# RWKV-7 recurrence and a gelu MLP on one core: a new order for tasks 157 to 655 of a hand-written list

## The chip, the cores and the metric

The kernel runs on one core of a Trainium2 chip, in float32. The metric is device time in microseconds; before and after are compared by the median of their runs. The engines are TensorE (PE, with its weight loads as PEld), VectorE (DVE), ScalarE (ACT), GpSimd (POOL) and SyncE (SP), which issues nearly all transfers.

## The reference

For 4 batches and 8 heads, a 40 x 40 state is carried through 768 steps; the outputs of all heads, brought to 3072 tokens of 320 channels, pass through an MLP of width 2048 with the quick gelu.

```python
for t in range(S):
    y[:, :, t] = np.einsum('bhd,bhde->bhe', rt, state)
    Sa = np.einsum('bhde,bhe->bhd', state, at)
    state_decay = state * wt[:, :, None, :] - np.einsum('bhd,bhe->bhde', Sa, bt)
    state = state_decay + np.einsum('bhd,bhe->bhde', vt, kt)
...
h = x @ w_in
g = h * (1.0 / (1.0 + np.exp(-1.702 * h)))
return (g @ w_out)
```

## The kernel before

**Units and chunks.** Time is cut into 12 chunks of 64 steps. A unit is one chunk for two of the four batches, so there are 24 units; unit i is chunk i // 2. For each unit, `decay` (L548) makes running products of w by logarithm, sum and exponential, `prep` (L623) scales k, a, b and makes the score matrices A (L640) and RV (L652), `inverse` (L672) inverts a triangular system in five levels (`level`, L746, and for the first four units `plain_level`, L768), and `solve` (L846) takes the state in from two units before, solves (`solved`, L909), reads out y (`read`, L923) and makes the new state (`updated`, L940) and the unit's x (`decayed`, L956). x goes to DRAM (`part_with`, L971) and comes back transposed by its layout (`get_back`, L977). There is one buffer for x on its way out (L282), so a unit's x cannot be written before that of the unit before has landed in DRAM.

**The MLP.** Once both units of a chunk have come back, `mlp` (L987) multiplies by w_in (`up`, L990, ten tasks for each of four pairs q), applies gelu on ACT (`gelu`, L999), and multiplies by w_out (`down`, L1004, eight tasks for each of two halves). The MLP's matmuls are most of PE's work, and they serve as filler between the steps of the recurrence, which depend on one another. But the MLP of chunk 0 cannot begin before units 0 and 1 are done.

**The weights.** w_in and w_out arrive as 64-bit words in eight slices (L441), four transfers each. Each slice is put together by one pass on ACT (`rebased`, L455), three on DVE (`bounded`, `shifted`, `rounded`, L459 to L467) and one on POOL (`joined`, L471), through a few staging places that are used again. Slices 0 to 3 serve `up` of q 0 to 3, slices 4 to 7 serve `down`.

**The order.** Every step is a task; the program numbers them as it makes them (L65). In which order they are emitted, and so the order of each engine's own queue, is a list written out in `ORDER` (L109 to L246). A token is the task's number, the letter of its engine (p PE, a ACT, d DVE, g POOL, s SP) and a digit: for tasks that use PSUM, which of the four pairs of banks they use (L295), for transfers, how many may be under way (the window, L332; 0 for any number). `listed` (L89) reads the list and marks where ACT must load another activation table (L102). An engine works its queue in order and waits where an input, a buffer or a PSUM pair is not ready. Two engines that read one PSUM tile do so one after the other. All matmuls carry line L301, all transfers on SP line L331, whichever task they belong to.

The tasks that the prediction speaks of, by number:

| task | what it is |
|---|---|
| 139, 140 | x of unit 0 to DRAM, and back |
| 189, 190, 191, 193 | unit 1: X (`solved`), its mask to M, y (`read`), x (`decayed`) |
| 194, 195 | x of unit 1 to DRAM, and back |
| 344 | RV's load for unit 3, window 2 |
| 53, 60 | pieces of w_out |
| 319, 351, 353, 360, 363, 302 | B0 of unit 2, A3 and RV3 (scores of unit 3), L11 and L13 (levels 0 and 1 of unit 3), L18 (last level of unit 2) |
| 196 to 205, 207 to 216 | `up` of chunk 0, q 0 and q 1 |
| 330, 331 and 400, 401 | x of units 2 and 3 to DRAM, and back |
| 552 | wc's load for unit 8, into the buffer that unit 5's exponentials read |
| 82, 549 | `rebased` of the last slice; exponentials of unit 5 |
| 570, 571, 537 | preset of PT for unit 5; N5 (its scores); B1 of unit 4 |
| 498, 578, 503 | L20, L21, L22: levels 0 of units 4 and 5 and level 1 of unit 4 |
| 610, 566, 694 | zT of unit 5; A5; sums over time of unit 6 |
| 402 to 411 | `up` of chunk 1, q 0, the first that need x of unit 3 |

Of the kernel before, what the change touches and what calls it, by code (L numbers as in the profile page):

```python
# [109 lines left out]
0s 8s 1s4 5s 102a 7s 6s 3a 9s 157a 87p0 88p1 10s 89a1 100p2 90a0 95d 13s4 4a 11s 93d 12s 101d2 98p3 2s 94d 97d 17s 103p1 16s 96d  # L110
142p0 15s 104a1 105d1 141p2 143a0 106d 99d3 107p1 144a2 18s4 148g 132p3 108a1 109d1 155p0 45s4 149d 27s 150g 156d0 158p2 14s4
110p1 159a2 160d2 91s4 130p0 161d 19a 24s4 112d1 162p2 111a1 22d 26s4 25s 163a2 113p1 20d 131a0 152g 164d2 34s4 92a 272s 21d
165p0 114a1 151g 271s 147a 153p2 115d1 273s 166a0 167d0 116p1 23g 28a 154d2 262p0 343s 117d1 263p2 133a3 342s 264a2 118d1 168p3
36s 31d 33s 119p1 276g 169a3 170d3 35s 120d1 42s 122a1 171p2 277d 278g 121a 43s 124d1 123a1 126p3 173d2 125a1 127d3 285a 29d
128p1 172a2 44s4 286p3 30d 54s4 37a 174p2 129d1 32g 51s4 288d3 134p1 178a2 146s4 175d2 145s 265a0 135d1 176a 187p0 289d 136p1
275s4 179a2 266g 61s 38d 138d1 188a0 341s 139s 287a3 181p0 39d 185p3 40d 137a1 177a2 290p1 313d 180a2 182a0 53s4 280g 279g 274s
186a3 183p2 292d1 281p0 291a1 333p3 41g 184d2 332p1 282d0 189p2 334a3 60s4 345s 314p0 190d2 316a0 346d 355a 191p3 347d 315d0
193d3 356p2 344s2 62s 140s 194s 195s4 192d3 293p0 335a1 358d2 46a 283p3 359d 317p1 294a0 295d0 349g 318a1 284d3 360p0 269a 348d
350g 296p1 336d 361a0 362d0 319p3 383d 357a2 297a1 298d1 384p0 321p2 49d 320a3 299p1 385a0 47d 322a2 63s4 363p3 300a1 301d1
323d2 386a0 302p1 364a3 365d3 353p0 351p2 306a1 48d 267s3 207p3 52s3 307a1 305d1 208p3 50g 268s3 64a 303d1 209p3 352d2 210p3  # L120
211p3 354d0 308a1 196p2 304a 212p3 65d 197p2 213p3 72s3 214p3 70s3 270d 55a 309p1 337s3 198p2 69s4 366p0 310a1 66d 199p2 367a0
# [120 lines left out]
2677p0 2653a3 2654p2 2655p2 2656p2 2657p2 2658p2 2659p2 2660p2 2661p2 2662p2 2663p2 2678p0 2664a2 2665p1 2666p1 2667p1 2668p1  # L242
2669p1 2670p1 2671p1 2672p1 2673p1 2674p1 2679p0 2675a1 2680p0 2681p0 2682p0 2683p0 2687p3 2684d0 2685d0 2688p3 2686s 2689p3
2690p3 2691p3 2692p3 2693p3 2694p3 2698p1 2695a3 2699p1 2696d3 2700p1 2697s 2701p1 2702p1 2703p1 2704p1 2705p1 2706d1 2707d1
2708s
# [904 lines left out]
```

## Time and profile before

| | us |
|---|---|
| median of three runs (lowest to highest) | 680.3 (678.17 to 682.07) |
| span of the profiled execution | 677.7 |
| PE busy | 649.6 |
| DVE busy | 449.7 |
| ACT busy | 329.1 |
| POOL busy | 175.7 |

The profile is of one execution. The page gives its span, from the first to the last instruction, and no separate time for what lies around it. An engine's busy time is the time in which at least one of its instructions ran. The groups "idle before, releaser" tell how long an engine had been idle and what ended that. In a row of the timeline stand the start, the time until the last of the merged instructions ended, engine, line, operation, tiles, shape, count, and in brackets the idle time before it. In a row of the waits stand who waited, for whom, the sum in us, how often, and the longest. In the view by stretches a row holds the stretch, its length, and each engine's busy time, then the granted TensorE clock, the DMA engines' busy share and GB/s.

### The profile page before, as it was taken

What the parts mean: (1) busy time and instruction counts of PE and PEld (TensorE: products, weight loads), DVE (VectorE), ACT (ScalarE), POOL (GpSimd) and SP (SyncE); (2) the same over time, 40 slices, a digit from 0 to 9 for tenths busy, and PEclk for the clock granted to TensorE, in tenths of its full rate; (3) what the DMA queues carried; (4) which work ended last, traced back from release to release, by engine and by line L of the source; (5) the groups of instructions that cost most, each with busy time, mean ns of one, the idle gap of its engine ahead of it and who ended that gap; (6) DMA issues with size and microseconds to landing.
All of it is one profiled execution on the core that took longest, in us unless ns stands there. A gap on an engine that the chain in (4) does not pass through costs nothing.

```text
span 677.7 us, 42447 instructions
## 1 busy us (share of the span) xinstructions
PE 649.6 (96%) x19616; PEld 568.7 (84%) x19616; DVE 449.7 (66%) x916; ACT 329.1 (49%) x681; POOL 175.7 (26%) x201
## 2 busy tenths in 40 slices
PE   5777999999999999999999999999999999999997
PEld 4667787787999997888888899999889798799896
DVE  5777779777867668757776687868656766675001
ACT  3676745634564655654545445455344454263010
POOL 6541443324123123123113211322411421300000
PEclk9979999999999999999999999999999999999999
DMA  6875753415324314432404513513412411200200
GB/s 208 295 255 160 226 172 97 129 42 152 107 64 131 94 58 124 114 107 65 124 14 131 149 35 108 155 33 107 140 38 62 130 53 45 69 15 14 60 13 21
DMA packets 35473, 69.74 MB, mean 103 GB/s; under 512 B 5472, under 2 KB 14816, under 8 KB 35296
## 3 DMA queue, kind: packets, MB, share of 16 engines
q1 hardware_dynamic: 35216, 66.99, 32.9%
q8 instruction: 154, 2.52, 1.6%
q14 instruction: 23, 0.19, 0.1%
q10 hardware_dynamic: 80, 0.04, 0.0%
HBM read 59.15 MB, written 7.86 MB: 99 GB/s over the span
## 4 chain that ended last, share of the span: by engine, by line
PE 88%; DMA 6%; DVE 2%; issue 1%; SPq 1%; ACT 1%; DVEq 0%; ACTq 0%
PE ps_up L301 31%; PE ps_down L301 29%; PE ps_level L301 8%; PE ps_y L301 5%; PE ps_B L301 4%; PE ps_X L301 2%; PE ps_N L301 2%; PE ps_rz L301 1%; PE ps_RV L301 1%; PE ps_A L301 1%; PE ps_zT L301 1%; SPq L331 1%; DMA w_sb<-in_w_in 1%; PE ps_cum L301 1%; PE ps_T L301 1%
## 5 line engine op out<-in xcount | busy, mean ns | idle before, releaser
L301 PE MATMUL ps_up<-xT_all,w_sb 64*64 64x256 f32 x3840 | 253.3, 377 | 2.1 <-issue 1.3
L301 PE MATMUL ps_down<-w_sb,g 64*64 64x320 f32 (+1 forms) x3200 | 241.5, 419 | 0.2 <-ACT zr L879 0.2
L301 PEld LDWEIGHTS ps_up<-xT_all,w_sb 64*64 64x64 f32 x3840 | 170.8, 133 | 18.8 <-issue 2.1
L301 PEld LDWEIGHTS ps_down<-w_sb,g 64*64 64x64 f32 x3200 | 142.5, 133 | 31.6 <-issue 0.4
L1000 ACT ACTIVATE g<-ps_up 128x1024 f32<-128x1024 f32 x48 | 49.2, 1025 | 46.3 <-PE ps_up L301 45.8
L719 POOL TENSOR_TENSOR EX<-ES,quads 128x512 f32<-128x512 f32 x30 | 39.7, 1324 | 116.4 <-DVE ES L712 77.7
L761 ACT COPY W<-ps_level 128x512 f32<-128x512 f32 x56 | 32.8, 585 | 67.7 <-PE ps_level L301 66.0
L301 PEld LDWEIGHTS ps_level<-W,EX 64*64 64x64 f32 x2560 | 60.0, 134 | 5.4 <-DVE T L840 0.2
L763 DVE TENSOR_TENSOR E<-two,ps_level 128x256 f32<-128x256 f32 x80 | 33.1, 415 | 36.5 <-ACT W L761 32.3
L301 PE MATMUL ps_level<-W,EX 64*64 64x64 f32 (+1 forms) x2560 | 56.8, 217 | 0.0
L717 ACT ACTIVATE EX<-ES,quads 128x256 f32<-128x256 f32 x82 | 37.2, 501 | 31.9 <-DVE ES L712 31.3
L629 POOL TENSOR_TENSOR ak<-ak,FT 128x512 f32<-128x512 f32 x17 | 23.0, 1353 | 77.2 <-DMA ak<-in_ak 54.4
L301 PEld LDWEIGHTS ps_level<-PT,EX 64*64 64x64 f32 x1280 | 30.7, 138 | 11.5 <-DVE EX L733 3.3
L301 PE MATMUL ps_level<-PT,EX 64*64 64x64 f32 (+2 forms) x1280 | 32.5, 234 | 6.9 <-DVE EX L733 5.0
L712 DVE STREAM_TRANSPOSE ES<-E 128x256 f32<-128x256 f32 x80 | 35.3, 443 | 4.4
L301 PE MATMUL ps_y<-RV,kh 64*64 64x104 f32 (+1 forms) x768 | 35.4, 247 | 0.9 <-DVE M L917 0.9
L301 PE MATMUL ps_y<-M,bh 64*64 64x104 f32 (+1 forms) x768 | 35.5, 247 | 0.7 <-DVE M L917 0.5
L901 ACT COPY B<-ps_B 128x416 f32<-128x416 f32 (+1 forms) x35 | 17.2, 493 | 34.4 <-PE ps_B L301 34.2
L301 PEld LDWEIGHTS ps_y<-RV,kh 64*64 64x64 f32 x768 | 29.6, 133 | 3.2 <-DVE M L917 1.5
L917 DVE TENSOR_TENSOR M<-ps_X,later 128x832 f32<-128x832 f32 (+1 forms) x24 | 23.9, 995 | 10.2 <-PE ps_X L301 10.0
L301 PE MATMUL ps_B<-RV,A 64*64 64x104 f32 (+1 forms) x768 | 29.2, 252 | 0.8 <-issue 0.8
L637 POOL TENSOR_TENSOR kh<-time,G 128x320 f32<-128x320 f32 x18 | 16.2, 901 | 51.2 <-PE ps_y L301 34.6
(133 smaller groups left out, 1099.0 us busy)
## 6 DMA issues: line engine op xcount, KB each, us to landing
ak<-in_ak SPq DMA_DIRECT2D x48, 160.0 KB
rv<-in_rv SPq DMA_DIRECT2D x48, 160.0 KB
time<-in_time SPq DMA_DIRECT2D x24, 320.0 KB
xT_all<-x_dram SPq DMA_DIRECT2D x48, 160.0 KB
wc<-in_wc SPq DMA_DIRECT2D x20, 264.0 KB
logw<-in_w SPq DMA_DIRECT2D x24, 160.0 KB
RV<-in_v SPq DMA_DIRECT2D x24, 160.0 KB
b<-in_b SPq DMA_DIRECT2D x48, 80.0 KB
```

What stands on the lines that cost most here:

```text
L301: nc.tensor.matmul(o, lhsT, rhs, start=start, stop=True, skip_group_check=True)
L331: begun.append(queue.dma_start(dst, src).ins)
L629: plan.add(R, {"DVE": 690.0, "POOL": 1270.0, "sbuf": True}, lambda t: of(t.engine).tensor_mul(ahT(), ahT(), FT_of(i)), reads=T("ak", "FT") ...
L637: plan.add(R + 4, {"POOL": 870.0, "DVE": 490.0, "sbuf": True}, lambda t, n=n, dst=dst: of(t.engine).tensor_mul(dst(i)[:, :, :D], by_head(t ...
L712: plan.add(rank, dve(256), lambda t: nc.vector.transpose(ES(n), source(t)), writes=[key("ES", n, 6)], **reads)
L717: nc.scalar.activation(dst[:, :, h], ES(n), ACT.Copy, scale=quads[:, h, :1])
L719: of(t.engine).tensor_mul(dst, ES(n).unsqueeze(2).to_broadcast([128, 8, 2, 32]), quads.unsqueeze(1).to_broadcast([128, 8, 2, 32]))
L761: plan.add(rank, any2(512), lambda t: copy(t.engine)(tiles_of(W(n + 1)), blocks(psum(t, ""), 64)), writes=[key("W", n + 1, 5)], pair=pair)
L763: plan.add(rank, dve(256), lambda t: nc.vector.tensor_sub(tiles_of(E(n + 1)), every(two32, [128, 2, 4, 32]), blocks(psum(t, ""), 64)[:, :, ...
L901: plan.add(R, any2(4 * wide), lambda t: copy(t.engine)(dst(), some(psum(t, "")[:, :, :208])), writes=[("Bv", i)] if x and c > 0 else T("B" ...
L917: plan.add(R + 1, dve(8 * wide), lambda t: nc.vector.tensor_tensor(M_of(i)[:, :, :wide].rearrange("p (j b) n -> p b j n", b=2), some(psum( ...
L1000: plan.add(-45, {"ACT": 1030.0, "table": "gelu"}, lambda t: nc.scalar.activation(g_of(c * NQ + q).rearrange("p m r n -> p r m n"), psum(t, ...
```

## The change

Only `ORDER` differs. The same tasks stand in it; up to place 156 and from place 656 on the list is what it was. In between, 495 places hold another token: tasks come earlier or later in their engine's queue, the transfers on SP too, 47 tasks run on another engine that can do them, and 132 more use another PSUM pair. No transfer has another window. The rest of the diff is lines broken elsewhere; the new list is two lines longer, so every line behind it has a number higher by 2 in the kernel after. The lines that hold the changed places:

```diff
-275s4 179a2 266g 61s 38d 138d1 188a0 341s 139s 287a3 181p0 39d 185p3 40d 137a1 177a2 290p1 313d 180a2 182a0 53s4 280g 279g 274s
-186a3 183p2 292d1 281p0 291a1 333p3 41g 184d2 332p1 282d0 189p2 334a3 60s4 345s 314p0 190d2 316a0 346d 355a 191p3 347d 315d0
-193d3 356p2 344s2 62s 140s 194s 195s4 192d3 293p0 335a1 358d2 46a 283p3 359d 317p1 294a0 295d0 349g 318a1 284d3 360p0 269a 348d
-350g 296p1 336d 361a0 362d0 319p3 383d 357a2 297a1 298d1 384p0 321p2 49d 320a3 299p1 385a0 47d 322a2 63s4 363p3 300a1 301d1
-323d2 386a0 302p1 364a3 365d3 353p0 351p2 306a1 48d 267s3 207p3 52s3 307a1 305d1 208p3 50g 268s3 64a 303d1 209p3 352d2 210p3
-211p3 354d0 308a1 196p2 304a 212p3 65d 197p2 213p3 72s3 214p3 70s3 270d 55a 309p1 337s3 198p2 69s4 366p0 310a1 66d 199p2 367a0
-200p2 58d 468p1 201p2 368d0 469a 473s 202p2 476s 203p2 67d 387p0 477s 470a1 490d 204p2 68g 480s 339a 205p2 369p1 388d0 206a2
-215p3 371d1 218p0 219p0 56d 472s4 216p3 483g 71s4 220p0 217a3 471d 81s4 221p0 482d 79s 311p2 222p0 370a1 223p0 224p0 312d2 225p0
-340d 372p3 229p1 478s4 376a3 230p1 57d 378a3 324p2 560s4 377a3 59g 226p0 78s4 375a3 325d2 231p1 73a 232p1 227p0 373d3 326p2 374d
-228a0 389p3 484g 479s3 327d2 338s4 240p0 529d 390a3 481g 328d2 379p3 233p1 380a3 329d 234p1 391p2 485g 241p0 556s4 392d2 80s4
-242p0 393d2 74d 486p3 235p1 487d3 530p2 236p1 75d 531a2 381p3 237p1 532a2 330s4 382d3 238p1 76d 491p2 394p3 494a2 493d2 77g
-239a1 243p0 395d3 82a 488p1 557s3 396p3 489d1 474a 558s4 83d 331s 251p1 492d2 495d 252p1 84d 85d 253p1 398d3 86g 559s4 548p2
-244p0 703s 397d3 549a 570d 553s 245p0 496d 550a2 552s 399d 497a 254p1 551g 554a 498p3 564d 400s 568p2 565g 499a3 246p0 569d2
-500d3 563g 247p0 562d 694p2 561g 255p1 248a0 401s2 249d0 475d 256p1 250s 533p3 257p1 534a3 555d 695a 571p0 535p3 573d0 258p1
-574a0 698s4 501d 696a2 609d 502g 536a3 537p2 572d0 259a1 576d 566p3 538a2 702s 402p0 575g 567d3 577a 403p0 404p0 539d2 785s3
-700a 405p0 706s 708d 406p0 578p3 407p0 580d3 408p0 260d1 610p2 409p0 581d 709g 410p0 611d2 411p0 612d2 503p1 707d 582g 412a0
-424p2 425p2 504d1 704s2 426p2 505d1 427p2 697d 428p2 579d3 613p1 701d 429p2 614a1 583p0 430p2 584a0 506d 431p2 585d0 432p2 507a
-782s2 586d 433p2 587d 446p3 434a2 508p1 588p0 509a1 447p3 590d0 589a0 510d1 261s2 413p2 511d 699s 414p2 591d 512a 783s 415p2
-592g 416p2 513p0 417p2 514a0 515d0 593p1 516d 418p2 594a1 595d1 419p2 596d 420p2 517a 597d 421p2 422p2 518p0 423a2 435p1 519d0
-436p1 521d0 520g 437p1 522d0 438p1 523d0 439p1 440p1 524d0 525p2 716p0 526a2 441p1 717d0 927s 442p1 718d0 527p2 443p1 719d0
-444p1 528d2 598p0 721d 445a1 540p2 720d 722g 601d0 603a0 617p1 602d0 541d2 448p3 618a1 604d0 542p2 619d1 599d0 600d 615p1 705s
-544d2 449p3 616a1 781s 710d 545g 711d 605p0 723p1 606a0 450p3 607p0 451p3 546s 608d0 930s 452p3 725d1 724d1 620p0 726d 543d2
-727a 773p1 453p3 621d0 778s 774a 547s 754d 728p2 622p0 454d3 455d3 729d2 456s 457p3 775a1 776g 730d2 784s 786g 779a 777s 624d0
...
+136p1 275s4 179a2 266g 61s 38d 138d1 188a0 341s 287a3 181p0 185p3 180a2 274s 46a 177a2 290p2 182d0 186a3 183p0 355a 137a1
+184d0 291a2 279g 280g 292d2 313d 345s 189p1 333p3 332p0 190d1 334a3 281p2 47d 191p1 314p3 139s 336g 48d 282d2 140s 335a0 347d
+293p0 193d1 192a1 315d3 294a0 194s 62s 316d3 317p2 295d0 49d 318a2 296p3 283p1 383d 298d3 346g 356p0 39d 358d0 284d1 63s4
+297a3 357a0 299p2 300a2 301d2 384p0 321p1 349g 322a1 323d1 50g 359d 195s4 207p3 319p2 269a 208p3 385d0 320d2 386d0 60s4 360p1
+209p3 267s3 302p0 348g 53s4 196p2 69s4 362d1 40d 305a0 477s 361a1 306a0 52s3 197p2 210p3 211p3 351p1 212p3 213p3 344s2 308a0
+303d0 350d 307a0 352d1 304a 270d 476s 363p0 309p1 365d0 214p3 310d1 364d0 70s3 64a 215p3 198p2 199p2 353p1 200p2 55a 201p2
+468p0 71s4 354d1 268s3 72s3 366p1 469a 216p3 41g 202p2 203p2 470a0 67d 58d 368d1 65d 56d 557s3 337s3 66d 471d 367a1 204p2 68g
+387p0 388a0 217a3 205p2 79s 490a 369p1 206a2 218p0 219p0 220p0 370d1 371d1 338s4 78s4 558s4 221p0 222p0 223p0 224p0 81s4 225p0
+73a 311p1 226p0 312d1 372p3 227p0 228a0 229p1 57d 375a3 230p1 478s4 480s 482d 324p2 231p1 232p1 481d 377a3 74d 80s4 325d2
+376a3 378a3 472s4 560s4 391p0 59g 392a0 373d3 233p1 234p1 393d0 75d 483d 76d 235p1 491p3 389p0 326p2 236p1 374a 390a0 237p1
+339a 240p0 493d3 494d3 328d2 570a 238p1 77g 241p0 492d3 496d 379p3 327d2 479s3 529d 239a1 486p2 329g 82a 380d3 251p1 381p3
+242p0 340d 495d 485g 382d3 487d2 243p0 484d 83d 84d 530p3 532a3 531a3 394p2 395d2 252p1 244p0 85d 548p2 549a 488p3 556s4 86g
+497a 489d3 550a2 253p1 396p3 498p2 562d 245p0 561g 552s 246p0 564g 398d3 397d3 500d2 499a2 571p3 330s4 247p0 572d3 573d3 331s
+551d 565g 575d 399d 706s 559s4 400s 401s2 576d 533p2 254p1 534a2 474a 574a3 537p2 248a0 255p1 568p3 577g 249d0 501d 538d2 609d
+539d2 256p1 473s 578p0 535p2 257p1 580d0 536d2 579a0 610p0 569d3 502g 503p2 505d2 506d 250s 258p1 504d2 563g 611a0 402p3 612a0
+694p0 403p3 475d 259a1 404p3 702s 695a 260d1 703s 566p2 697d 696a0 405p3 406p3 407p3 408p3 424p1 409p3 553s 507a 425p1 567d2
+581d 508p2 582d 426p1 509d2 583p0 410p3 427p1 585d0 700a 411p3 510d2 428p1 511d 584d0 429p1 699s 586d 587d 413p2 412a3 704s2
+414p2 512a 708d 430p1 613p0 261s2 701d 588p3 415p2 590d3 589d3 431p1 432p1 591d 614a0 433p1 446p3 416p2 434a1 417p2 592d 707g
+513p1 554a 593p0 515d1 514d1 595d0 516d 517a 594d0 698s4 596d 418p2 419p2 420p2 435p1 436p1 437p1 518p0 421p2 422p2 782s2
+423a2 438p1 439p1 519d0 521d0 520g 440p1 441p1 525p2 442p1 443p1 523d0 522d0 555d 524a0 597d 716p0 526a2 719a0 527p2 709g
+718d0 717d0 528d2 444p1 447p3 445a1 598p0 721d 601d0 540p1 617p2 602d0 722d 604d0 448p3 599d0 449p3 618a2 603a0 720d 615p0
+619d2 541d1 542p2 600a 605p1 544d2 545g 450p3 710d 711g 616a0 606a1 723p1 607p0 451p3 608d0 725d1 724d1 452p3 785s3 781s 783s
+546s 620p0 726d 543d2 727a 773p1 453p3 621d0 774a 754d 930s 778s 547s 728p2 622p0 454d3 455d3 729d2 457p3 775a1 456s 927s 705s
+776g 730d2 784s 786g 779a 777s 624d0 458p3 623d0 625g 731d 793p1 833d 732a 459p3 733p2 789g 460p3 626s 734a2 794d1 735d2 714p0
```

More of the change, by code (lines that the diff above doesn't have):

```diff
@@ L242 @@
[L242 to L245, printed above, removed]
+0s 8s 1s4 5s 102a 7s 6s 3a 9s 157a 87p0 88p1 10s 89a1 100p2 90a0 95d 13s4 4a 11s 93d 12s 101d2 98p3 2s 94d 97d 17s 103p1 16s
@@ L246 @@
+2675a1 2680p0 2681p0 2682p0 2683p0 2687p3 2684d0 2685d0 2688p3 2686s 2689p3 2690p3 2691p3 2692p3 2693p3 2694p3 2698p1 2695a3
+2699p1 2696d3 2700p1 2697s 2701p1 2702p1 2703p1 2704p1 2705p1 2706d1 2707d1 2708s
 """
```

220 lines of the change are left out of this document (111 added, 109 removed).

## The prediction

> **What bounds the kernel now.** I read the page's busy shares and slices first, then busy time by stretches of the span, then TensorE's waits in the stretches that the change touches, then the transfers there one by one.
>
> ```profile
> span 677.7 us, 42447 instructions
> PE 649.6 (96%) x19616; PEld 568.7 (84%) x19616; DVE 449.7 (66%) x916; ACT 329.1 (49%) x681; POOL 175.7 (26%) x201
> PE   5777999999999999999999999999999999999997
> PE 88%; DMA 6%; DVE 2%; issue 1%; SPq 1%; ACT 1%; DVEq 0%; ACTq 0%
> ```
>
> TensorE (PE) is busy for 96% of the span and is 88% of the chain that ended last. Only the first four slices, 68 us, show it well below nine tenths. The other engines have room. So time is won only where PE stands idle, and that is early.
>
> Matching each engine's list with its instructions in the trace puts the first task that the change moves at 43.5 us and the last at 160 us. The view of busy time by stretches gives, in each row, the length and then PE, weight loads, DVE, ACT and POOL:
>
> ```profile
> 43.00:66.50 23.50, 17.80 (x817) 15.96 (x807) 18.05 (x35) 15.19 (x38) 6.52 (x5) 1.00 0.57 168
> 66.50:120.00 53.50, 52.08 (x1413) 41.93 (x1408) 43.96 (x72) 31.02 (x62) 24.54 (x15) 1.00 0.54 168
> 120.00:160.00 40.00, 39.65 (x1240) 31.63 (x1236) 28.63 (x66) 19.90 (x38) 9.57 (x10) 1.00 0.31 92
> 160.00:640.00 480.00, 478.56 (x14620) 424.51 (x14612) 327.88 (x693) 233.19 (x475) 113.12 (x123) 1.00 0.30 86
> ```
>
> PE is idle for 5.70 us before 66.5, for 1.42 us up to 120, for 0.35 us up to 160, and for 1.44 us in the 480 us after that. This has two consequences. All that a new order of these tasks can win by filling idle time is 7.5 us, 1.1%. And since PE is full from 160 us on and the list there is unchanged, what PE is ahead or behind at 160 us is what the end is ahead or behind.
>
> What ended PE's idle time, first before 66.5 us, then from 66.5 to 160 us:
>
> ```profile
> PE ps_level L301 <- DVE EX L733: 1.6, 2, 0.8
> PE ps_level L301 <- ACT zraw L946: 0.9, 1, 0.9
> PE ps_B L301 <- issue: 0.8, 1, 0.8
> PE ps_N L301 <- issue: 0.7, 1, 0.7
> PE ps_zT L301 <- DVE zr L855: 0.6, 1, 0.6
> ```
>
> ```profile
> PE ps_up L301 <- issue: 1.0, 2, 0.7
> PE ps_level L301 <- ACT EX L717: 0.3, 1, 0.3
> ```
>
> The first group is mostly the dependent chain of units 1 to 3: PE waits for a transpose or a copy on DVE or ACT, with nothing else in the list. The `issue` rows, 1.5 and 1.0 us, name no other engine; nothing that the list orders ends them. So 4.2 us of the first stretch and some 0.4 us of the second are what an order can aim at.
>
> **The change part by part.** The same 2709 tasks run; 495 places of the list hold another token. Counted in the diff: 47 tasks change engine (26 go to DVE, 20 leave it), 132 more change only their PSUM pair, no transfer changes its window.
>
> *The first up projections.* PE has filler only once x of units 0 and 1 is back from DRAM. SyncE's rows (the last four belong to units 2 and 3 and are used further down), the making of x of unit 1, the first `ps_up`, and a way back's time until it landed:
>
> ```profile
> 44.63 0.66 SPq L331 DMA_DIRECT2D x_dram<-x  x2
> ...
> 54.00 0.33 SPq L331 DMA_DIRECT2D RV<-in_v  x1
> 54.38 0.42 SPq L331 DMA_DIRECT2D extra<-in_w_out  x1
> 54.86 1.72 SPq L331 DMA_DIRECT2D xT_all<-x_dram  x2
> 56.67 0.84 SPq L331 DMA_DIRECT2D x_dram<-x  x2
> 61.39 1.09 SPq L331 DMA_DIRECT2D xT_all<-x_dram  x2
> ...
> 92.82 1.94 SPq L331 DMA_DIRECT2D x_dram<-x  x2
> ...
> 106.46 0.45 SPq L331 DMA_DIRECT2D wc<-in_wc  x1
> 111.85 0.68 SPq L331 DMA_DIRECT2D x_dram<-x  x2
> 114.04 1.13 SPq L331 DMA_DIRECT2D xT_all<-x_dram  x2
> ```
>
> ```profile
> 49.34 1.02 DVE L917 TENSOR_TENSOR M<-ps_X,later 128x832 f32<-128x832 f32 x1 [1.10 <-PE ps_X L301]
> ...
> 52.43 0.86 DVE L962 TENSOR_TENSOR x<-ps_y,FT 128x128 f32<-128x128 f32 x4
> ```
>
> ```profile
> 66.48 0.81 PE L301 MATMUL ps_up<-xT_all,w_sb 64*64 64x256 f32 x9
> ```
>
> ```profile
> 487.81 3.94 DMA xT_all<-x_dram
> ```
>
> x of unit 1 is ready at 52.43 + 0.86 = 53.3, but is sent at 56.67, because an RV load with a window of two (54.00), a weight piece (54.38) and unit 0's way back (54.86) stand ahead of it. The new list puts that RV load and two weight pieces (tasks 344, 53, 60) behind the way back of unit 1, and unit 0's way back straight after its sending. By the send of unit 1 (56.67 to 61.39: 4.7 us until landed), unit 0's way back is then free to go at 44.63 + 4.7 = 49.3. x of unit 1 itself moves little. `solved` is taken ahead of three PE tasks and M comes some 0.3 to 1 us earlier, but between M and x, where DVE now spends 2.1 us on other tasks (50.36 to 52.43), the new list puts two weight passes, the mask of A and a product, by my estimate 3 us. I take 53.0. Sent at 53.0, landed 57.7, fetched by 57.7 + 3.9 = 61.6. In before the same sum gives 61.4 + 3.9 = 65.3, and PE came to it at 66.48 after other work.
>
> That is 4.9 us earlier for the first up, but not 4.9 us won, because six tasks that ran ahead of it (levels L11, L13, the last level L18, A3, RV3, B0 of unit 2) now come behind. Their cost when PE is not waiting, from the chain that ended last:
>
> ```profile
> 65.73 0.47 PE ps_RV L301 x32
> 66.20 0.47 PE ps_A L301 x32
> ...
> 72.39 0.88 PE ps_level L301 x40
> ...
> 82.45 0.69 PE ps_level L301 x40
> 84.00 0.71 PE ps_X L301 x32
> ```
>
> 2 x 0.88 + 0.69 + 0.47 + 0.47 + 0.7 (B0 has the 32 matmuls of X) = 4.1 us. So the new order does at 61.6 + 4.1 = 65.7 what the old one had done at 66.48, **0.8 us earlier**, provided that the interleaved ups hide the moved levels' copies; ten `up` tasks each of q 0 and 1 lie between them, so they should. Bounds: with a landing as quick as the 2.2 us of unit 3's sending (111.85 to 114.04), 2.5 us more; with DVE's 3 us of passes all in x's way and nothing gained before, 1 us lost.
>
> *From there to 160 us.* The chain that ended last leaves PE once more here, for DVE, on the way to level L20 of unit 4, which waits for this EX:
>
> ```profile
> 105.78 2.41 DVE PT L414 x2
> ...
> 108.57 0.92 ACT EX L717 x2
> ```
>
> The copy that presets PT (L414) moves to ACT, 49 places earlier; B1 of unit 4, N5, L20, L21, L22 come 15 to 33 places earlier with `down` tasks behind them. So this chain gets ahead while PE still has filler, and the 0.3 us wait for EX goes. Of the `issue` gaps I cannot say whether they come again. Bounds: nothing, or all of 1.42 + 0.35 = 1.8 us. No row decides; I take the middle, **0.9 us**.
>
> *What covers the rest.* DVE gets some 3 us more in 117 us (an estimate from the durations of the tasks that change hands); it is busy for 43.96 of 53.50 us in its fullest stretch, so it carries this, but at 82% there, any wait on it is passed on. The order on ACT alternates more between exponentials and gelu: 33 changes of the table in the list, 29 before. Each is one row like this:
>
> ```profile
> 76.68 1.28 ACT L1000 ACT_TABLE_LOAD   x1
> 77.98 1.02 ACT L1000 ACTIVATE g<-ps_up 128x1024 f32<-128x1024 f32 x1
> ```
>
> Four more are 4 x 1.28 = 5.1 us of ACT. Each stands ahead of an activation that waits for PE (g of pair 3, exponentials of unit 5), ACT is free for 22.5 of 53.5 us, and a load needs no operand, so I cost them at nothing. Without that cover, they cost 5.1 us. The Trainium skill, ScalarE: Activation LUTs, section What ACT_TABLE_LOAD costs, puts a switch at about 1283 ns and 1380 ns of drain, 2.66 us. The trace agrees with the load and shows no drain: gelu begins 0.02 us after the load's end. By the page the four would be 10.6 us of ACT, still less than its idle time.
>
> **The sum.** 0.8 + 0.9 = 1.7 us less than the profiled span of 677.7: 676.0. The page gives no time for what lies around the span; the median of the three runs, 680.3, is 2.6 us above it, and I keep that distance: **678.6 us**.
>
> **The rivals.** *The whole gain.* The moved levels find filler everywhere, and the waits on DVE and ACT before 66.5 go too: 4.2 + 0.4 us, and some of the slow starts: 5 us, **675.3**. For it speaks that all those waits have up tasks nearby in the new list. Against it, that nothing can be filled before x is back at about 61.6, and most of the 4.2 us lie before 60.
>
> *The idle time only moves.* What is won at the first up is lost in the denser DVE list, near **680.3**. DVE's 82% in the second stretch speaks for it.
>
> *x of units 2 and 3 comes too late (slower).* The last four of SyncE's rows above are units 2 and 3; here are the making of unit 3's x and the first up that needs it:
>
> ```profile
> 108.47 3.36 DVE L962 TENSOR_TENSOR x<-zr,FT 128x128 f32<-128x128 f32 x4
> ```
>
> ```profile
> 120.35 1.91 PE L301 MATMUL ps_up<-xT_all,w_sb 64*64 64x256 f32 x32
> ```
>
> The sending of unit 2 (92.82) moves behind the `wc` load of unit 8 (106.46). That load waits for ACT's exponentials of unit 5, which stand behind a weight pass that waits for the last piece of w_out. x has one buffer, so unit 3's x waits for that sending to land. With the exponentials done near 103 (my estimate, some 3 us ahead of the 106.46 that follows them now), unit 2 is sent at 103.3, landed between 105.5 and 108.0 (2.2 to 4.7), x of unit 3 is made in 0.9 to 3.4 us, but not before DVE has N5, near 109: 110 to 112.4. It is fetched 2.2 to 4.7 us later and 3.9 us after that landed: 116 to 121. PE, 1.7 us ahead but with L21, L22 and zT of unit 5 put before it and A5 and the sums of unit 6 behind (some 0.7 us more by the steps above), comes to it near 119.3. Until then it costs nothing; after that PE stands still one for one, since the next ups all need it, and the lead is used up at 121. If the weight piece is some 4 us late, unit 3 lands at up to 125 and the kernel is 4 us slower: **684.3**.
>
> *The table loads are not hidden.* All four on the path: 5.1 - 1.7 = 3.4 us over 680.3, **683.7**. ACT's waits for PE speak against it.
>
> **How the numbers follow.** Forecast (a gain of 0 to 3.7 us, 676.6 to 680.3): 0.48. The whole gain: 0.19. The idle time only moves: 0.13. x too late: 0.15. Table loads: 0.05. About 0.5%, 3.4 us, is what a measurement of this kernel can tell from no change. Faster by more than that: the whole gain and 0.05 of the forecast's edge, 0.24. Slower: x too late, the table loads' larger half, and 0.02 of the moved idle time, 0.20. Within: 0.56. The range reaches from the whole gain with some of the other idle time, 674.3, to just under x too late, 683.8; it leaves out some 0.2.
>
> **What would show it.** Right: the first `ps_up` near 62 us and x of unit 1 sent near 53; PE's idle time before 66.5 us near 4.5 to 5; the first up of chunk 1 (120.35 above) near 119 with no wait for `xT_all`; 33 table loads, each followed by a wait for PE. Wrong: x of unit 1 sent after 55; PE waiting for `xT_all` before 120 us; PE's idle time between 66.5 and 160 us above 3 us; any lead at 160 us that is gone at the end.

## The result, and the profile after

The changed kernel takes 684.66 us (median of 6 runs, 682.43 to 687.95) against 679.82 us before (6 runs, 678.17 to 682.07): a ratio of 1.0075, 95% interval 1.0052 to 1.0099. Timed again later on another chip it was 1.0048 (1.0022 to 1.0073). So the new order costs about 4 us, where I had forecast a gain of 1.7.

The page of the profiled execution (687.95 us, the slowest of the six), the lines that answer to those shown of before, and the row of TensorE's granted clock:

```profile
span 686.2 us, 42443 instructions
PE 655.7 (96%) x19616; PEld 570.1 (83%) x19616; DVE 452.3 (66%) x915; ACT 330.5 (48%) x682; POOL 177.4 (26%) x203
PE   5777989999999999999999999999999999999997
PEclk9978999999999999999999999999999999999999
PE 90%; DVE 4%; issue 2%; DMA 2%; ACT 1%; SPq 0%; DVEq 0%; ACTq 0%
```

Each slice is 17.2 us. The sixth slice of PE, 86 to 103 us, is 8 where it was 9. And PE is busy 6.1 us longer for the same 19616 matmuls, with the clock down to 8 in the fourth slice: its matmuls ran slower. The view by stretches of the same kernel (stretch, length, busy time of PE, weight loads, DVE, ACT, POOL, then the granted clock, DMA share and GB/s):

```profile
43.00:66.50 23.50, 16.06 (x640) 14.29 (x644) 17.62 (x30) 10.54 (x27) 9.90 (x7) 0.94 0.59 187
66.50:120.00 53.50, 49.76 (x1384) 42.16 (x1380) 39.42 (x60) 31.42 (x61) 21.29 (x13) 0.93 0.42 127
120.00:160.00 40.00, 39.47 (x1170) 32.67 (x1164) 32.49 (x72) 21.85 (x43) 8.28 (x6) 1.00 0.30 91
160.00:640.00 480.00, 478.47 (x14772) 414.36 (x14775) 333.21 (x704) 237.60 (x484) 115.87 (x128) 1.00 0.29 89
```

PE is idle for 7.44 us before 66.5 (before: 5.70), then for 3.74 (1.42) and 0.53 (0.35), and the clock is 0.94 and 0.93 where it was 1.00. From 160 us on nothing has changed. TensorE's waits in these stretches, first before 66.5, then to 160 us:

```profile
PE ps_zT L303 <- ACT P L704: 1.7, 1, 1.7
PE ps_level L303 <- issue: 1.6, 2, 0.9
PE ps_A L303 <- issue: 1.1, 1, 1.1
PE ps_level L303 <- DVE EX L735: 1.0, 1, 1.0
```

```profile
PE ps_y L303 <- issue: 2.0, 1, 2.0
PE ps_N L303 <- DVE ES L714: 1.3, 1, 1.3
PE ps_B L303 <- DVE B L906: 0.5, 1, 0.5
```

Three rows are new or much larger: 1.7 us for zT of unit 3 (zT(3) from here on, and so with the others), 1.3 us for N(4), and 2.0 us in the middle of y(2) for nothing that the profile names; such a halt of PE is called a stand below.

**Where the first two come from.** zT(3) waits for ACT's copy of N(3), which comes behind DVE's copy of it. The timeline of DVE and that of POOL around them:

```profile
59.55 0.72 DVE L735 STREAM_TRANSPOSE EX<-ps_level 128x512 f32<-128x512 f32 x1
60.19 2.73 DVE L467 TENSOR_SCALAR w_sb<-w_sb 128x1280 int32<-128x1280 int32 x1
62.84 0.68 DVE L728 TENSOR_TENSOR PT<-ps_N,within 128x512 f32<-128x512 f32 x1
```

```profile
59.11 3.13 POOL L475 TENSOR_TENSOR w_sb<-w_sb,extra 128x1280 int32<-128x1280 int32 x1 [3.48 <-DVE extra L471]
```

The pass on L467 (`shifted` of weight part 2, task 39) takes 2.73 us. In before the same task stood 51 places earlier and took 0.82 us (`44.52 0.82 DVE L465`). It ends 0.68 us after POOL's join of part 3 ends (59.11 + 3.13 = 62.24; 60.19 + 2.73 = 62.92): it stood until the join was done. N(3) had been ready at 60.7. Some 30 us later the same happens to ahT of unit 4 (task 481, on L631; the change moved it from POOL to DVE) beside the join of part 4:

```profile
90.12 3.45 DVE L631 TENSOR_TENSOR ak<-ak,FT 128x512 f32<-128x512 f32 x1
93.50 0.81 DVE L463 TENSOR_SCALAR w_sb<-w_sb 128x1280 f32<-128x1280 f32 x1
94.23 1.01 DVE L919 TENSOR_TENSOR M<-ps_X,later 128x832 f32<-128x832 f32 x1
95.17 0.43 DVE L714 STREAM_TRANSPOSE ES<-ps_level 128x256 f32<-128x256 f32 x1
```

```profile
89.68 3.34 POOL L475 TENSOR_TENSOR w_sb<-w_sb,xT_all 128x1280 int32<-128x1280 int32 x1 [2.43 <-DVE w_sb L467]
```

3.45 us, to 0.55 us past the join's end at 93.02; behind it come M(2), whose X was done at 91.4, and ES23 (task 373), which frees the PSUM pair that N(4) needs. A DVE pass that reads PSUM is not held: M(1) in before ran its usual 1.02 us in the middle of a join. The Trainium skill, SBUF — State Buffer, section SBUF: two separate sides, says that GpSimd and VectorE, where a pass of VectorE runs in a two-port mode or has two inputs in SBUF, share one pair of ports as an exclusive lock: whichever starts first has it for its whole instruction, and the other blocks. The trace agrees, with 0.68 and 0.55 us between the join's end and the pass's.

In all 20 profiles together, worked out from their instructions, DVE began 60 passes from SBUF to SBUF (transposes left out) with 0.35 us or more of a join still to run. All 60 were held, and ended 0.15 to 0.69 us after the join; none of the 289 passes that read PSUM was, nor were three transposes from SBUF to SBUF (0.45 us, their usual time). Before had such holds too (a `bounded` pass took 1.78 us beside the join of part 3), and PE waited behind one of them: PT's presets for unit 5, two copies of some 0.29 us, took 2.48 us beside a join that ended at 107.82, and this is the 2.41 us of `PT` in the chain that the prediction shows.

```profile
105.70 2.48 DVE L414 COPY PT<-one 128x256 f32<-128x256 f32 x2
```

```profile
104.87 2.95 POOL L473 TENSOR_TENSOR w_sb<-w_sb,extra 128x1280 int32<-128x1280 int32 x1 [4.37 <-DVE extra L469]
```

**The clock.** Rows of the view by stretches, cut where the granted clock changes:

```profile
60.10:63.50 3.40, 1.73 (x69) 1.31 (x63) 3.40 (x4) 0.80 (x1) 3.40 (x2) 1.00 0.70 188
63.50:70.30 6.80, 6.32 (x144) 5.60 (x148) 3.99 (x8) 2.48 (x5) 0.54 (x1) 0.50 0.73 235
...
97.70:101.10 3.40, 1.36 (x49) 1.16 (x44) 1.24 (x4) 3.35 (x7) 2.81 (x1) 0.99 0.66 213
101.10:104.50 3.40, 3.40 (x35) 3.40 (x31) 2.26 (x5) 0.83 (x1) 2.84 (x6) 0.50 0.47 149
```

Where PE was busy for 1.73 and 1.36 of 3.40 us, it worked at half the clock for the next 6.8 and 3.4 us: 5.1 us lost on top of the waits. All falls of the clock in all profiles of this case, but for those that the end cuts off, are 3.4 us long or a multiple of it.

**A ledger.** From the end of y(0), the last PE task ahead of the change, to the end of the first `up` tasks behind it (task 641): the time, PE's idle time and what ended most of it, and the time at half clock, worked out from the instructions and the clock of each trace (three profiles of the changed kernel, two of before; e and x are the repairs below):

```
              stretch  idle  issue  ACT  DVE  half clock
before          145.4   7.7    2.9  1.6  2.7      0.0
before again    143.1   5.7    1.3  2.0  2.2      3.4
changed         153.1  11.7    4.7  2.8  4.2     10.2
changed again   150.0  10.5    5.9  2.4  2.0      4.3
changed, third  149.3  10.9    3.7  4.0  3.0      3.4
e1 (39)         147.0   6.9    2.5  0.1  4.3      7.6
e2 (481, 74)    144.9   6.6    2.5  1.1  2.5      4.1
e3 (both)       147.4  10.8    7.1  1.6  2.1      0.0
x1 (transfers)  150.2  11.5    4.3  3.5  3.4      3.4
x1 again        149.8  10.2    4.1  2.6  3.3      7.8
x2 (x1 and e2)  146.6   7.9    3.1  2.8  1.8      3.5
x2 again        147.1   7.4    2.1  3.5  1.6      6.8
x3 (x1 and e3)  145.7   6.6    3.0  0.6  3.0      6.8
```

Means: before 144.3, changed 150.8, so 6.5 us; idle time is 4.3 of it (11.0 - 6.7), and half of 4.3 us more at half clock, 2.1, the rest. The timed loss is smaller, 4 us: two of the three profiled executions of the changed kernel took longer than its median, and both of before took less. The granted clocks of the timed executions put the clock's part lower too: (1 - granted clock) x span is 6.8 us in mean over 18 executions of the changed kernel and 5.7 us over 117 of before, a difference of 1.1 us, good to 1.2.

### The profile page after: what moved, and what is told of

Same layout as the page of the kernel before. It is cut to its first block, busy times and chain, and to the rows that moved or that the text cites. A ratio compares the mean times of both kernels' runs of the same rounds, so it can differ in the third digit from the quotient of the medians.

```text
span 686.2 us, 42443 instructions
## 1 busy us (share of the span) xinstructions
PE 655.7 (96%) x19616; PEld 570.1 (83%) x19616; DVE 452.3 (66%) x915; ACT 330.5 (48%) x682; POOL 177.4 (26%) x203
## 3 DMA queue, kind: packets, MB, share of 16 engines
q8 instruction: 154, 2.52, 1.5%
## 4 chain that ended last, share of the span: by engine, by line
PE 90%; DVE 4%; issue 2%; DMA 2%; ACT 1%; SPq 0%; DVEq 0%; ACTq 0%
PE ps_down L303 30%; PE ps_up L303 30%; PE ps_level L303 9%; PE ps_y L303 5%; PE ps_B L303 5%; PE ps_X L303 2%; PE ps_N L303 2%; PE ps_A L303 2%; PE ps_rz L303 1%; PE ps_RV L303 1%; PE ps_zT L303 1%; PE ps_T L303 1%; PE ps_cum L303 1%; PE ps_Q L303 1%; DMA b<-in_b 1%
## 5 line engine op out<-in xcount | busy, mean ns | idle before, releaser
L303 PEld LDWEIGHTS ps_down<-w_sb,g 64*64 64x64 f32 x3200 | 139.9, 134 | 32.4 <-ACT zr L881 0.4
L763 ACT COPY W<-ps_level 128x512 f32<-128x512 f32 x52 | 30.4, 585 | 71.0 <-PE ps_level L303 63.2
L721 POOL TENSOR_TENSOR EX<-ES,quads 128x512 f32<-128x512 f32 x28 | 37.0, 1324 | 103.1 <-DVE ES L714 69.5
L303 PEld LDWEIGHTS ps_level<-W,EX 64*64 64x64 f32 x2560 | 57.5, 135 | 7.0 <-issue 1.0
L303 PE MATMUL ps_level<-W,EX 64*64 64x64 f32 (+1 forms) x2560 | 55.2, 218 | 0.5 <-issue 0.5
L631 POOL TENSOR_TENSOR ak<-ak,FT 128x512 f32<-128x512 f32 x18 | 24.4, 1356 | 81.0 <-DMA ak<-in_ak 53.3
L303 PEld LDWEIGHTS ps_level<-PT,EX 64*64 64x64 f32 x1280 | 32.3, 146 | 13.8 <-issue 4.4
L303 PE MATMUL ps_level<-PT,EX 64*64 64x64 f32 (+2 forms) x1280 | 34.8, 244 | 8.0 <-issue 3.5
L303 PEld LDWEIGHTS ps_B<-RV,A 64*64 64x64 f32 x768 | 26.3, 143 | 4.8 <-PE ps_level L303 0.6
```

The source lines that it names most:

```text
L303: nc.tensor.matmul(o, lhsT, rhs, start=start, stop=True, skip_group_check=True)
L631: plan.add(R, {"DVE": 690.0, "POOL": 1270.0, "sbuf": True}, lambda t: of(t.engine).tensor_mul(ahT(), ahT(), FT_of(i)), reads=T("ak", "FT") ...
L721: of(t.engine).tensor_mul(dst, ES(n).unsqueeze(2).to_broadcast([128, 8, 2, 32]), quads.unsqueeze(1).to_broadcast([128, 8, 2, 32]))
L763: plan.add(rank, any2(512), lambda t: copy(t.engine)(tiles_of(W(n + 1)), blocks(psum(t, ""), 64)), writes=[key("W", n + 1, 5)], pair=pair)
```

## The experiments

Theory A: DVE's passes beside POOL's joins make PE wait, and the clock doubles the price. Rivals: B, the new order of the transfers; C, the reordering ahead of 85 us; D, chance; later E, late instructions. The kernels of the experiments have before's line numbers. Each edit but w's is one of the list.

**e1, e2, e3: the held passes moved.**

```diff
-... 39d 358d0 284d1 63s4 ...
+... 358d0 284d1 39d 63s4 ...
```

```diff
-... 481d 377a3 74d 80s4 325d2 ... 59g 392a0 373d3 ...
+... 377a3 80s4 325d2 ... 59g 392a0 373d3 481d 74d ...
```

> The changed kernel (684.66 us; before 679.82), with one VectorE pass moved: the `shifted` pass of weight part 2 (task 39) goes from ahead of PV11's copy of N(3) to behind RV(2), so that it is no longer begun while GpSimd joins weight part 3 (in the profile after it took 2.73 us there instead of 0.82, and N(3)'s copies, which were behind it, came 1.9 us late). Theory A (the pass is held up by GpSimd, TensorE waits 1.67 us for zT(3), and the granted clock then falls to 0.5 for 6.8 us): the wait at zT(3) goes, no half-clock stretch begins at 63.5 us, and the time falls by 1.7 + 3.4 = 5.1 us, to about 679.5 us. Theory A without the clock (the fall of the clock has another cause): 1.7 us, about 683.0 us, and the half-clock stretch is still there. Rival B (the new order of the transfers, or late instructions of TensorE, cost the time): no change, 684 to 685.5 us.

> The changed kernel with the other held-up pass moved: ahT(4) (task 481, 3.45 us beside GpSimd's join of weight part 4, 0.7 us usual) and `bounded` of part 6 (task 74) go behind M(2) and ES23, so that ES23 frees N(4)'s bank in time. Theory A: the 1.34 us wait of TensorE at N(4) goes, and where the wait was what led to the half-clock stretch at 101.1 us (3.4 us long, 1.7 us lost), that goes too: 681.6 to 683.3 us. Rival B: no change, 684 to 685.5 us.

> The changed kernel with both moves (tasks 39; 481 and 74). Theory A with the clock: the savings add, 5.1 + 1.3 to 3.0 us, so 676.5 to 678.3 us, a little below the kernel before. Theory A without the clock: 3.0 us, 681.7 us. Rival B: no change, 684 to 685.5 us.

Measured, against before on the same chip (680.34): e1 684.05, ratio 1.0073 (1.0045 to 1.0101); e2 681.24, 1.0030 (1.0008 to 1.0052); e3 682.33, 1.0043 (1.0018 to 1.0069). The wait at zT(3) is gone in e1, task 39 is back at 0.82 us, and the time has not moved: for this hold theory A fails. e2 takes back 2 to 3 us, with N(4)'s wait gone:

```profile
PE ps_y L301 <- issue: 1.1, 1, 1.1
PE ps_B L301 <- DVE B L904: 0.5, 1, 0.5
PE ps_level L301 <- issue: 0.5, 1, 0.5
```

e3 is between them (all three intervals overlap), not at 676.5 to 678.3: the savings do not add.

**e4: the new transfers alone.** Before's lists on four engines, the changed kernel's on SyncE.

> The kernel before with SyncE's queue alone in the changed kernel's order (all transfers of the stretch, their limits on transfers under way included); TensorE, VectorE, ScalarE and GpSimd run before's order word for word. Theory A (the loss is in the order on VectorE): as before, 679 to 681.5 us. Rival B (the transfers' order costs the time: it holds back x of units 2 and 3 or the instructions of TensorE): most of the 4.8 us, 683 to 685 us.

694.67 us, 1.0231 (1.0202 to 1.0261), beyond either theory. TensorE's waits say why:

```profile
PE ps_cum L301 <- ACT QT L826: 4.7, 1, 4.7
PE ps_rz L301 <- DVE E L763: 4.5, 1, 4.5
```

Two waits of 4.5 us and more that neither kernel has: before's lists with transfers that were ordered for another list. It tells nothing of what the transfers cost in their own list, so B stayed open.

**s1, s2, s3: the change cut in two.** New places up to a cut and before's order behind it, or the reverse.

> Places 156 to 309 in the new order, all that remains in before's order (39 is held up beside the join of part 3 here too; ahT(4) is on GpSimd again, ahead of nothing that waits). Two earlier runs (39 moved: 684.05; 481 and 74 moved: 681.24; both: 682.33; changed 684.66, before 680.3) say that the wait at N(4) costs 2 to 3 us in the end and the one at zT(3) about nothing. Theory A, so corrected (the loss is mostly ahT(4)'s, behind place 309): 680 to 682 us. Rival C (the loss is the reordering ahead of 85 us: TensorE's idle time there and the clock behind it): 683.5 to 685 us.

> Places 156 to 309 in before's order, all that remains in the new order; ahT(4) runs on VectorE beside GpSimd's join of part 4. Theory A, corrected: the wait at N(4) is there, 682.3 to 683.5 us. Rival C: as before, 679.5 to 681 us.

> Places 156 to 339 in the new order and the rest in before's, so that T21(2)'s buffer does not meet gelu(0) as it did in the earlier cut at 310; ahT(4) runs on GpSimd as in before. The second part alone (cut at 310) gave +2.4 us of the 4.8. If the first part carries the rest: before's 680.3 + 2 to 3 us, 682.3 to 683.5 us, with the wait at zT(3) and the stands in the first 65 us. If the first part costs nothing by itself: 680 to 681.5 us.

s2 is 682.50, 1.0035 (1.0014 to 1.0057), with N(4)'s wait (1.33 us) and a stand in y(2) (1.89 us): 2.4 us (good to 1.5) belong to places 310 to 655 alone, as theory A said, and against C as the whole cause. The first parts could not be had clean: s1 is 1.0139 (1.0107 to 1.0170) with a wait of 5.2 us for T21(2)'s buffer, s3 1.0088 (1.0060 to 1.0117) with 3.2 us for M(2), and neither kernel has these waits. What the first part costs by itself is not shown.

```profile
PE ps_T L301 <- ACT g L1000: 5.2, 1, 5.2
```

**before_again, after_again: chance.** The same two kernels, profiled once more.

> The kernel before once more, for a second profile of it: in its first one TensorE stood 0.32 us in the middle of L(5), at 30 us, with no wait shown; in the changed kernel and three variants of it, whose lists are the same up to there, 1.1 to 3.1 us. If such stands (at every 256th instruction of TensorE) come by chance, this profile shows one of 1 to 3 us there too, and its first 45 us are 1 to 5 us longer than in the first profile; if they belong to the changed program, it shows 0.3 us again.

> The changed kernel once more, for a second profile of it. Theory A: zT(3) waits about 1.7 us and N(4) about 1.3 us again, since VectorE's passes meet GpSimd's joins by the order and not by chance; the stand inside y(2) (2.04 us) and the half-clock stretches may differ from run to run. Rival D (chance alone): other waits.

The second profile of before stands 2.32 us in L(5), where the first stood 0.32; its first 45.9 us are 2.2 us longer, and its next stretch 2.3 us shorter. So a stand's size there is chance, and the first 45 us of all these kernels vary by 5 us. Against D: the changed kernel again waits 1.55 us at zT(3) (task 39: 2.73 us) and stands in y(2), 1.22 us; N(4) waits 0.48. Its third profile has 1.67, 1.77 and 1.31. In the two profiles of before zT(3) waits 0.56 us and not at all, N(4) does not wait, and y(2) has no stand.

**What a stand is.** The row without a cause, 2.0 us in y(2), comes five matmuls ahead of the task's end, with the operands of the matmuls before it. Number through all that TensorE's queue holds: matmuls, weight loads and the semaphore instructions between them. Then all the `issue` rows of a third of a microsecond and more in the profiles of before and after lie at 194 + a multiple of 256 (give or take one): 1218, 1986, 2242, 2498, 4802. In all 20 profiles, 121 of the 122 such rows of 0.3 us and more do; the other is one of 1.48 us in w. The page of the changed kernel has a queue that fits:

```profile
q8 instruction: 154, 2.52, 1.5%
```

2 x 19616 matmuls and weight loads, with the 295 semaphore instructions, fill 154 blocks of 256, and 2.52 MB in 154 packets is 16.4 KB each: TensorE's instructions come in blocks of 256, each as one packet. Read packet by packet, where PE stood, a packet starts up to 4.9 us after the block ahead of it is entered, takes 0.9 to 1.7 us, and PE went on 1.2 to 1.7 us after its end. In the changed kernel the block that ends in y(2) holds the last matmuls of an `up`, then N(4), B0(3) and y(2) with no `up` among them. From N(4) on, PE runs it in some 2.9 us; the packet of the next block starts 2.6 us after N(4) does, takes 0.95, and 1.3 us later PE goes on.

**x1, x2: the transfers.** SyncE's queue is held from 77 to 87 us by wt(7), the four transfers of the last weight slice (tasks 79, 78, 81, 80), whose room POOL's join of part 5 frees at 87.25, and ten tasks' transfers are pressed into 87 to 98 us. x1 puts these four behind the other six (the expectation counts seven); x2 has e2's edit too.

```diff
-... 79s ... 338s4 78s4 558s4 81s4 ... 478s4 480s ... 80s4 ... 472s4 560s4 ...
+... 338s4 558s4 ... 478s4 480s ... 472s4 560s4 79s 78s4 81s4 80s4 ...
```

> The changed kernel with four transfers moved on SyncE's queue: wt(7)'s (tasks 79, 78, 81, 80), which wait for GpSimd's join of weight part 5 and hold the queue from 77.2 to 87.3 us, go behind the seven transfers of units 4 to 6 that stand behind them and were pressed into 87 to 98 us. Theory E (TensorE's instructions come in blocks of 256 as transfers of their own, and one that is asked for while the DMA engines are full starts late: 4.55 us at 93.7 us, and TensorE then stands 2.04 us inside y(2)): the stand at y(2) falls below 1 us, and the time by 1 to 3 us with the clock, to 682 to 683.7 us. Theory A (the VectorE passes alone): no change, 684 to 685.5 us.

> The same with ahT(4) and `bounded` of part 6 behind M(2) and ES23 as well (alone that gave 681.24 against before's 680.34). Theories A and E together: 679 to 680.5 us, no slower than before. Theory A alone: 681 to 682 us.

x1: 1.0014 (0.9990 to 1.0038). x2: 0.9996 (0.9970 to 1.0023). These were on a chip on which before took 684.34, so I put them beside the changed kernel on one chip, with a fourth that also moves task 39.

> The changed kernel, timed beside the three repairs on one chip: 0.5 to 1.0% above before, as the first time (1.0075).

> The changed kernel with wt(7)'s transfers behind those of units 4 to 6, once more. If the held queue carries most of the loss: 0.0 to 0.3% above before, 0.4% or more below the changed kernel beside it. If the earlier 1.0014 was the other chip's: 0.5 to 0.8% above before.

> With ahT(4) and `bounded` of part 6 behind M(2) and ES23 as well. If both causes act at the same place (N(4) and y(2), 95 to 101 us) and are all of the loss: -0.2 to 0.2% against before. If (a) is nothing: 0.2 to 0.4% above, as with (b) alone (1.0030).

> With the `shifted` pass of part 2 (task 39) out of the way of GpSimd's join of part 3 too. If the hold at zT(3) costs what its wait and the clock behind it would say (1.7 to 3.4 us): 0.25 to 0.5% below x2. If, as in the two earlier pairs, it costs nothing in the end: as x2, within 0.1%.

```
changed   684.26   1.0048 (1.0022 to 1.0073)
x1        682.84   1.0033 (1.0010 to 1.0055)
x2        682.45   1.0019 (1.0000 to 1.0037)
x3        680.91   0.9997 (0.9976 to 1.0018)   before 680.50
```

With all three out, the loss is gone, and PE's idle time reads as in before (23.50 - 18.11 = 5.39, then 1.31 and 0.12), though the clock fell in the first stretch (0.83):

```profile
43.00:66.50 23.50, 18.11 (x669) 16.38 (x670) 16.97 (x31) 11.89 (x31) 9.31 (x7) 0.83 0.58 180
66.50:120.00 53.50, 52.19 (x1548) 44.63 (x1536) 42.21 (x74) 32.65 (x65) 25.11 (x16) 1.00 0.50 152
120.00:160.00 40.00, 39.88 (x1188) 33.33 (x1192) 30.50 (x66) 21.94 (x43) 7.50 (x9) 1.00 0.31 92
```

To within 1.5 us, the new order is then worth nothing and costs nothing. Each repair by itself, from the three pairs of kernels that differ in it alone (the changed kernel, x1 and x2 as means of their two timings): the transfers -0.38, -0.23 and -0.46%, mean -0.35; ahT(4) and `bounded` -0.32, -0.30 and -0.16%, mean -0.26; task 39 +0.12, +0.13 and -0.11%, mean +0.05. By the intervals above a mean is good to about 0.17%: 2.4 and 1.8 us, and nothing for task 39, each to 1.2 us.

**w: what a wait costs.** The kernel before; ahead of the pass that folds T21(i) into T, DVE copies T21(i) to a spare tile several times, which adds work and changes no output.

```diff
+            for _ in range(4 * (8 <= i < 13) + 6 * (13 <= i < 18) + 8 * (18 <= i < 23)):
+                nc.vector.tensor_copy(spare, psum(t, "")[:, :, :128])
```

> The kernel before with fifteen waits of TensorE put in, some 28 us apart: ahead of the pass that folds T21(i) into T, VectorE copies T21(i) to a spare tile 4 times for units 8 to 12, 6 times for 13 to 17, 8 times for 18 to 22 (about 0.45 us each; X(i) waits for the fold). Waits of about 1.3, 2.2 and 3.1 us. If a wait costs itself alone, the time rises by the sum of the waits, about 33 us or less where TensorE makes none up, and the granted clock stays at 1. If TensorE's clock falls to half after a stretch of 3.41 us in which it was busy for less than about half, as the profiles so far read: no fall for units 8 to 12, some for 13 to 17, most for 18 to 22, each 1.7 us more, 8 to 14 us on top of the waits.

44 us more than before (728.30 against 684.34; ratio 1.0638, 1.0584 to 1.0692). PE's idle time behind 200 us is 32.7 us, 31.5 more than in before, and there are seven falls of the clock, each 3.4 us long: 7 x 1.7 = 11.9, in all 43.4. Thirteen of the fifteen places show a wait of more than a microsecond. All five waits of 2.9 us and more led to a fall, two of the three of about 2 us did, none of the shorter ones. One of the smaller ones, with what follows it, and one of the larger:

```profile
419.35:422.10 2.75, 0.74 (x33) 0.77 (x37) 2.61 (x8) 0.58 (x1) 0.00 (x0) 1.00 0.00 1
422.10:425.50 3.40, 3.40 (x44) 2.55 (x37) 2.93 (x5) 0.00 (x0) 0.00 (x0) 0.51 0.02 5
...
538.60:541.60 3.00, 0.46 (x34) 0.35 (x24) 2.79 (x8) 1.61 (x8) 0.00 (x0) 1.00 0.00 0
541.60:545.00 3.40, 2.95 (x48) 2.54 (x52) 2.57 (x5) 0.00 (x0) 0.00 (x0) 0.50 0.03 5
```

The third wait of about 2 us lay across the edge of two such windows and cost itself alone. The Trainium skill, TensorE: Matmul & The Clock Gate, Part 1, tells of a free-running window of 3413 ns and of half the clock after an idle one. The window's length agrees. That a window must be idle doesn't: of the 3732 windows at full clock in all profiles of this case (the last 11 us of each left out), the clock fell after all 33 in which PE was busy for up to 46%, after 16 of 104 between 47 and 68%, and after none of 3595 above. Among those left out at the end there is one of 41% after which it did not fall.

**q1, r1: fewer transfers under way.** Same order, ten transfers limited to 2 (q1: the changed kernel's from 77 to 98 us; r1: before's from 22 to 31 us).

```diff
-79s 338s4 78s4 558s4 81s4 478s4 480s 80s4 472s4 560s4
+79s2 338s2 78s2 558s2 81s2 478s2 480s2 80s2 472s2 560s2
```

> The changed kernel, the ten transfers that SyncE begins between 77 and 98 us limited to 2 under way (eight had 4 or no limit); order as it was. Theory E: the instruction packet asked for at N(4) starts within 2.5 us instead of 3 to 4.6, the stand inside y(2) (2.04, 1.22, 1.77 us in three profiles) falls below 0.8 us, and the time by 1 to 2 us, ratio about 1.0035 to 1.005 (changed kernel 1.0075 and 1.0048). Rival (the stand has nothing to do with the transfers): 1.2 to 2 us again. Rival (data come late with fewer under way): a wait for units 4 or 5 and a longer time.

> The kernel before, ten transfers that SyncE begins from 22 to 31 us (weights 1 and 2, ak, b, rv of units 2 and 3) limited to 2 under way instead of 4 or any number. Theory E: the stand in L(5) (0.32 and 2.32 us in two profiles of this kernel, 0.9 to 3.1 in the others) falls below 0.8 us, the half-clock stretch behind it gets shorter, and the time falls by 1 to 4 us, ratio 0.994 to 0.9985, which would be below both kernels. Rival (data come late): TensorE waits for units 2 and 3, ratio 1.0 or more. Rival (stands by chance): no difference, 0.9985 to 1.0015.

q1: 684.17, 1.0050 (1.0021 to 1.0078), the changed kernel's time, and y(2) stands 1.50 us. The packet did start sooner, as E said, 1.8 us after N(4) for 2.6, with the DMA engines busy for 43% of the time since the block ahead was entered (80% in the changed kernel). But it took 1.2, and PE went on 1.35 us later: 4.3 us, for a block that PE ran in 2.8. So a lower load did not remove the stand at y(2): even so the block of small matmuls is shorter than the way of a packet. r1: in L(5) the packet starts 1.3 us after the block ahead is entered and there is no stand. E foresaw that, but for a lower load, and the DMA engines were busy for 97% of these 1.3 us; in the two profiles of before it was 86% of 1.2 us and 60% of 3.6. So load does not set the delay in L(5), and what sets it is not shown. The data that the limit holds back cost far more than a stand, 692.60, 1.0180 (1.0145 to 1.0215):

```profile
PE ps_B L301 <- ACT G L601: 9.8, 1, 9.8
```

No version came out clearly below before; x3 equals it.

## Why the prediction was wrong

**What bounds it: right.** PE from end to end; what it is behind at the end of the changed stretch (198.09 - 189.08 = 9.0 us in the two first profiles) it is behind at the end (8.5). Nothing here tests the ceiling of 7.5 us. But I read idle time as the whole price of a wait. The clock was in the page of before (`PEclk` has a 7 in its third slice), and I did not use it.

**The first up projections: the parts came out, the sum did not.** x of unit 1 was sent later than I said, 55.73 for 53.0, past the 55 that I had named as a sign, but landed quickly: its way back began at 57.90, against 57.7. Of the 2.7 us, 1.3 were there at the end of y(0) (44.99 for 43.66), ahead of the change.

```profile
46.83 0.68 SPq L333 DMA_DIRECT2D x_dram<-x  x2
50.68 1.17 SPq L333 DMA_DIRECT2D xT_all<-x_dram  x2
55.73 0.66 SPq L333 DMA_DIRECT2D x_dram<-x  x2
57.90 1.61 SPq L333 DMA_DIRECT2D xT_all<-x_dram  x2
```

By the same sum x was there at about 61.8 (57.90 + 3.9, an estimate). The first up came at 65.96, because PE stood at zT(3) until 63.98 and then worked at half clock. The step that failed first: the sum has PE at the first up as soon as x lands, and asks of the ups only that they hide the copies of what moved. zT(3) comes ahead of the first up and had no ups to hide N(3)'s copies. Counted from the end of y(0), the first up came after 21.0, 20.1 and 19.5 us in the three profiles of the changed kernel, and after 22.8 and 23.5 in before: 3.0 us earlier in mean, for 4.1 us of tasks put behind it. That is a loss of 1.1 us where the sum had a gain of 0.8.

**What covers the rest: the step that failed.** I wrote that DVE gets some 3 us more and carries this. I took the durations of the tasks that change hands from where they stood, and never asked what POOL did beside them where they were put. Held passes cost DVE 1.9 and 2.8 us in one piece each, ahead of copies that PE waited for. In the times, task 39's hold shows nothing; ahT(4)'s, with `bounded`, costs 1.8 us, and the held queue of transfers 2.4, each good to 1.2: two terms that my sum has at nothing. The rows that I showed of before had the mechanism in them. The 2.41 us of `PT` (105.78) are two copies of some 0.29 us, and the 3.36 us in which x of unit 3 is made (108.47) are four passes of 0.28, three of which end 0.15 us after a POOL pass. I asked of neither why it took so long. The table loads were hidden as I said: four more in the trace (34 for 30, one ahead of the list in each), and none of PE's waits above stands behind one.

**From there to 160 us: the wait for L20 went, as foreseen, and larger ones came.** Instead of the 0.9 us of gain stand N(4) (1.3 us), the stand in y(2) (2.0), and B of unit 4 (0.5). PE's idle time from 66.5 to 160 us is 4.27 us, beyond the 3 that I had named as a sign. I said of the `issue` rows that I could not tell whether they would come again; they are tied to every 256th instruction, so a new order decides which tasks share a block, and their mean went from 2.1 to 4.8 us.

**The rivals.** x of units 2 and 3 did come late, later than I worked out: sent at 114.59 and 122.02, not 103.3 and 112. PE never waited for it; it had other work. That rival's 684.3 us is close to the measured time by another mechanism, and confirms nothing. The mechanism that did it was not among my rivals. I had SyncE's list before me and followed only x; that wt(7) would hold the queue for 10 us I did not see.

**What stays open.** Why the transfers' repair is worth 2.4 us in the times, when the profiles of x1 show 0.7 us less at y(2) (0.95 in both, for 1.68 in mean) and a stretch 0.8 us shorter (150.0 for 150.8). It is not the clock: on the chip where all were timed together, (1 - granted clock) x span is 6.5 us in mean for the changed kernel and 7.3 for x1. Also open: why zT(3)'s hold costs nothing that the times show, although its wait is in every profile of the changed kernel (in the profiles of e1 and x3, without it, the clock fell all the same, at 60.1 and 57.7 us, for 6.8 us; that may be why); and what the first 150 places cost alone.

## What to carry to other kernels

Before a pass is moved on VectorE, look at what GpSimd runs beside its new place: two passes of 0.8 and 0.7 us became 2.7 and 3.5 us here, and everything queued behind them came late. A pass in the profile that takes several times as long as others of its kind is the sign of it. Price a wait of TensorE with the clock: here, if it took up more than about half of one 3.4 us window it cost another 1.7 us, and if not, mostly only itself. And when a queue of transfers is reordered, ask of each one what frees its room, since one that waits for a late release holds all behind it.

## What the runs showed of the hardware

- A VectorE pass from SBUF to SBUF, transposes left out, that begins beside a GpSimd join of 3 us ends 0.15 to 0.7 us after the join, in 60 of 60 cases (0.82 became 2.73 us, 0.7 became 3.45 and, in before, 0.29 became 2.28). All 289 passes that read PSUM ran their usual time.
- TensorE's instructions come 256 at a time in packets of 16 KB. A packet needs 3.4 us at the least here, where PE stood, from the entry of the block ahead of it until PE goes on (1.1 + 1.0 + 1.3), and up to 7.6 us (q1, at 37 us). PE stands when it runs a block faster, up to 3.1 us. The same stand varies from 0.3 to 3.1 us between executions.
- After a window of 3.41 us in which PE is busy for up to 46%, it works at half the clock for 3.4 us or a multiple of it; above 68%, never; between, after 16 of 104.
